# Cutting the first store of a streaming grouped 1x1 convolution into three parts

## The chip, the core and the metric

The kernel runs on one core of one Trainium2 chip. The metric is device time in microseconds (us) of that core. Five runs of the kernel before gave 477.75 to 478.17 us, with a median of 478.06 us.

## The reference

The input x has 512 x 512 pixels of 192 bfloat16 channels, in four groups of 48. Every group is multiplied by its own 48 x 48 matrix; the kernel size k is 1, so there is no neighbourhood and no padding.

```python
for i in range(k):          # k = 1
    for j in range(k):
        out = out + jnp.einsum('bhwgc,gcd->bhwgd',
                               xg[:, i:i+H, j:j+W, :, :], w[i, j])
```

So 100.66 MB are read and 100.66 MB are written, and there is little arithmetic for each byte.

## The kernel before

**Columns.** The pixels are laid out over 128 partitions. One "column" is one pixel in each partition: 384 bytes a partition, 49,152 bytes in all. There are about 2,050 columns. Four columns are a "group" (514 groups), two groups are a "pair" (257 pairs).

**Way of a group.** The SP queue loads columns into an input ring of 240 columns (`ring`). TensorE transposes a group in six blocks (L350) into `xT_ps`, VectorE copies a pair to `xT_sb` (L409), TensorE multiplies with block-diagonal weights (L370) into `o_ps`, and ScalarE (ACT) copies the group into an output ring of 280 columns, `oring` (L446). Stores go from `oring` to HBM and are issued by ACT too (L427), between two of its copies.

**Loads.** Loads are cut into pieces. The first three are 8, 24 and 48 columns (`HEAD`), and the later ones are mostly 80, that is 30,720 bytes a partition. SP waits on `t_done` until the transposes have freed the place in the ring (L318).

**Stores.** `plan_stores` cuts the output columns into stores whose ends lie on a grid of 72, 140, 212 and 280 columns of the ring (`OGRID`). For the last 240 columns the stores become smaller: 40 columns, and at the very end 24, 20, 16 and 8 (`LAST_PARTS`). The stores of the kernel before start with 72, 68, 72 and 68 columns. ACT issues a store while it handles a later group: at group g it first waits for the matmuls of g, then issues every store whose last group is at most g - 2 (L441), then waits for the store that last used this place in `oring` (L443), and then copies. So the first store of 72 columns (groups 0 to 17) is issued at group 19.

**Special fields.** At two places 48 columns are loaded and stored with uneven parts, some of them through the POOL queue (`PARTIAL`, `UNEVEN`), so that the 16 DMA engines get unequal shares. Nothing of this depends on the first store: POOL waits on `t_done`, and on `go_sem`, which ACT raises when it issues the stores of those fields.

**Queues.** Three queues feed the same 16 DMA engines: q1 (SP, the loads), q10 (ACT, the stores) and q0 (POOL, the uneven parts). A transfer over 128 partitions gives each engine 8 packets, one for each partition. Instructions are fetched over q8 and q14.

Of the kernel before, what the change touches and what calls it, by code (L numbers as in the profile page):

```python
# [1 line left out]

# [25 lines left out]
OGRID = (72, 140, 212, 280)  # L28
OCOLS = OGRID[-1]
HEAD = (8, 24, 48)  # L30
LATE_COLS = 240
LATE_PART = 40
LAST_PARTS = (24, 20, 16, 8)
# [50 lines left out]
def plan_fields(npix):  # L84

    parts, head = [], sum(HEAD)
    for slots, special in FRONT:
# [14 lines left out]
def plan_pieces(fields):  # L102
    pieces = []
    for f in fields:
        first = [f.cols]
        if f.full:
            first = list(HEAD) if not f.g0 and sum(HEAD) <= f.cols else []
        c = 0
# [7 lines left out]
def plan_stores(fields):  # L116
    total = 4 * fields[-1].g1
    stores, at = [], 0
    for f in fields:
        c = 0  # L120
        if not f.full and at + f.cols > OCOLS:
            at = 0
        ends = []
        if f is fields[-1] and f.cols > LATE_COLS:
            ends = [f.cols - sum(LAST_PARTS[i:]) for i in range(len(LAST_PARTS))]
        while c < f.cols:
            if f.full:
                end = min([g for g in OGRID if g > at + 24] or [OCOLS]) - at + c
                if f.cols < BIG:
                    end = min(OCOLS - at + c, f.cols)  # L130
                if ends and c >= f.cols - LATE_COLS:
                    end = min(OCOLS - at, LATE_PART) + c
                end = min([end, f.cols] + [e for e in ends if e > c])
            else:
                end = f.cols
            stores.append(Store(f, c, end, at))
            c, at = end, (at + end - c) % OCOLS
    return stores
# [40 lines left out]
def bass_standalone__grouped__vision_kernel(nc, x, w, out):  # L179
# [5 lines left out]
    fields = plan_fields(npix)  # L185
    pieces = plan_pieces(fields)
    stores = plan_stores(fields)
    units = plan_units(pieces)
    unit_of = {g: u for u in units for g in range(u.g0, u.g1)}
# [291 lines left out]
```

## Time and profile before

| what | value |
|---|---|
| median of 5 runs | 478.06 us (477.75 to 478.17) |
| the profiled execution | 478.44 us |
| its span, first to last instruction | 476.6 us, so 1.84 us lie around it |
| busy: PE, PEld, DVE, ACT | 432.2, 391.3, 246.8, 388.9 us |
| DMA queues q1, q10, q0, share of 16 engines | 48.0%, 47.8%, 3.3% |
| moved | 201.57 MB, 423 GB/s on the mean |
| granted TensorE clock | 0.971 on the mean |

A queue's share is the time that its packets took, summed over the engines and divided by 16 times the span. An engine works on one packet at a time, so these shares add up. The page's DMA line is the same in 40 slices of 11.9 us. A window's DMA share can be over 1.00, since a packet is counted in the window in which it starts.

### The profile page before, as it was taken

What the parts mean: (1) busy time and instruction counts of PE and PEld (TensorE: products, weight loads), DVE (VectorE), ACT (ScalarE), POOL (GpSimd) and SP (SyncE); (2) the same over time, 40 slices, a digit from 0 to 9 for tenths busy, and PEclk for the clock granted to TensorE, in tenths of its full rate; (3) what the DMA queues carried; (4) which work ended last, traced back from release to release, by engine and by line L of the source; (5) the groups of instructions that cost most, each with busy time, mean ns of one, the idle gap of its engine ahead of it and who ended that gap; (6) DMA issues with size and microseconds to landing.
All of it is one profiled execution on the core that took longest, in us unless ns stands there. A gap on an engine that the chain in (4) does not pass through costs nothing.

```text
span 476.6 us, 13580 instructions
## 1 busy us (share of the span) xinstructions
PE 432.2 (91%) x6178; PEld 391.3 (82%) x6178; DVE 246.8 (52%) x258; ACT 388.9 (82%) x515; POOL 12.5 (3%) x28
## 2 busy tenths in 40 slices
PE   4999999999698999999997997999978998996993
PEld 4988889888697898888897896898877987886882
DVE  2555555555354555555553553555535555552551
ACT  2898899988587998998894985999968987976883
POOL 1000000200002000000000000200002000000000
PEclk9999999999899999999997997999989999998998
DMA  8999999999999999999999999999999999999997
GB/s 324 442 384 428 441 426 430 436 418 436 439 430 424 435 420 438 437 429 425 441 432 429 429 431 431 431 430 422 435 441 419 433 422 424 440 424 432 420 419 291
DMA packets 10674, 201.57 MB, mean 423 GB/s; under 512 B 2112, under 2 KB 2112, under 8 KB 2752
## 3 DMA queue, kind: packets, MB, share of 16 engines
q1 hardware_dynamic: 4320, 97.44, 48.0%
q10 hardware_dynamic: 5120, 97.42, 47.8%
q0 software_dynamic: 1216, 6.49, 3.3%
q8 instruction: 9, 0.15, 0.1%
q14 instruction: 9, 0.07, 0.0%
HBM read 100.68 MB, written 100.66 MB: 422 GB/s over the span
## 4 chain that ended last, share of the span: by engine, by line
PE 48%; DMA 39%; ACT 9%; issue 1%; ACTq 1%; another core or an unknown queue 1%; SPq 0%; POOLq 0%
DMA out_dram<-oring 30%; PE o_ps L370 28%; PE xT_ps L350 20%; DMA ring<-in_x_dram 9%; ACT oring L446 9%; ACTq L427 1%; SPq L320 0%; SPq L313 0%; ACTq L420 0%; POOLq L300 0%; POOLq L299 0%; ACTq L429 0%
## 5 line engine op out<-in xcount | busy, mean ns | idle before, releaser
L446 ACT CAST oring<-o_ps 128x768 bf16<-128x768 f32 x514 | 387.6, 801 | 80.2 <-PE o_ps L370 56.6
L409 DVE COPY xT_sb<-xT_ps 128x1536 bf16<-128x1536 bf16 x257 | 246.2, 958 | 216.9 <-PE xT_ps L350 216.9
L370 PE MATMUL o_ps<-wt,xT_sb 128*128 128x144 bf16 (+1 forms) x3084 | 290.1, 237 | 26.5 <-ACT oring L446 21.0
L370 PEld LDWEIGHTS o_ps<-wt,xT_sb 128*128 128x128 bf16 x3084 | 213.7, 99 | 64.4 <-ACT oring L446 55.1
L350 PE MATMUL xT_ps<-ident,ring 128*128 128x128 bf16 x3084 | 223.1, 223 | 7.2 <-POOLq L300 3.9
L350 PEld LDWEIGHTS xT_ps<-ident,ring 128*128 128x128 bf16 x3084 | 190.9, 100 | 10.0 <-POOLq L300 4.1
L286 POOL DMA_DIRECT2D fill<-in_x_dram x8 | 4.6, 574 | 350.9 <-PE xT_ps L350 235.8
L296 POOL DMA_DIRECT2D ring<-in_x_dram x6 | 3.3, 559 | 0.0
L307 POOL DMA_DIRECT2D out_dram<-oring x6 | 3.3, 556 | 0.0
L332 PE MATMUL o_ps<-w_sb,esel 48*128 48x48 bf16 x10 | 0.6, 209 | 2.8 <-DMA w_sb<-in_w_dram 2.8
L332 PEld LDWEIGHTS o_ps<-w_sb,esel 48*128 48x128 bf16 x10 | 0.4, 111 | 2.7 <-issue 2.7
L402 DVE CAST wt<-o_ps 128x480 bf16<-128x480 f32 x1 | 0.7, 658 | 3.4 <-PE o_ps L332 3.4
L446 ACT ACT_TABLE_LOAD x1 | 1.3, 1283 | 0.8 <-PEq L466 0.8
L273 POOL TENSOR_SCALAR_AFFINE_SELECT esel<-esel 48x272 bf16<-48x272 bf16 x1 | 0.4, 402 | 0.0
L270 POOL MEMSET esel<- 48x272 bf16 x1 | 0.3, 318 | 0.3 <-POOLq L466 0.3
L277 POOL TENSOR_SCALAR_AFFINE_SELECT ident<-ident 128x128 bf16<-128x128 bf16 x1 | 0.3, 282 | 0.0
L271 POOL MEMSET ident<- 128x128 bf16 x1 | 0.2, 198 | 0.0
L466 POOL MEMSET const-float32-0.0<- 128x1 f32 x1 | 0.1, 98 | 0.3 <-issue 0.3
L466 POOL MEMSET const-bfloat16-1.0<- 128x1 bf16 x1 | 0.1, 101 | 0.0
L466 POOL MEMSET const-uint8-127<- 128x1 uint8 x1 | 0.1, 101 | 0.0
L466 POOL MEMSET const-float32-1.0<- 128x1 f32 x1 | 0.1, 98 | 0.0
## 6 DMA issues: line engine op xcount, KB each, us to landing
ring<-in_x_dram SPq DMA_DIRECT2D x22, 3840.0 KB, 26.8
out_dram<-oring ACTq DMA_DIRECT2D x11, 3456.0 KB, 41.3
out_dram<-oring ACTq DMA_DIRECT2D x10, 3264.0 KB, 41.5
out_dram<-oring ACTq DMA_DIRECT2D x3, 1920.0 KB, 19.6
out_dram<-oring ACTq DMA_DIRECT2D x1, 3840.0 KB, 47.5
ring<-in_x_dram SPq DMA_DIRECT2D x2, 1536.0 KB, 31.5
out_dram<-oring ACTq DMA_DIRECT2D x2, 1536.0 KB, 43.4
out_dram<-oring ACTq DMA_DIRECT2D x1, 2880.0 KB, 39.1
```

The lines of the kernel that those rows point to most:

```text
L273: gp.affine_select(out=esel[:], in_=esel[:], pattern=[[-1, ECOLS]], compare_op=AluOpType.is_equal, fill=0.0, base=ESHIFT, channel_multipli ...
L286: gp.dma_start(dst, src).then_inc(fill_sem[k], 16)
L296: gp.dma_start(sbuf, dram).then_inc(ld_sem[ld_key[p.i, n]], 16)
L307: gp.dma_start(dram, sbuf).then_inc(st_sem[i][n], 16)
L332: last = pe.matmul(o_ps[:, NOB - 1, col:col + CG], lhsT=esel[:, s0:s0 + 128], rhs=w_sb[:, g, :], start=True, stop=True, skip_group_check=True)
L350: last = pe.transpose(xT_ps[:, g % NXP, j * 128:(j + 1) * 128], xg[:, j * 128:(j + 1) * 128], ident[:])
L370: last = pe.matmul(o_ps[:, v % NOB, c0_:c1_], lhsT=xs[:, j * 128:(j + 1) * 128], rhs=wt[:, WOFF[tc]:WOFF[tc] + (c1_ - c0_)], start=(tc == ...
L402: dve.tensor_copy(wt[:], o_ps[:, NOB - 1, 0:WCOLS]).then_inc(wc_sem, 1)
L409: dve.tensor_copy(xT_sb[pair % NXS][:, 0:n * 2 * UC].rearrange("p (g c) -> p g c", g=n), xT_ps[:, b0:b0 + n, 0:2 * UC]).then_inc(e_done[pa ...
L427: act.dma_start(dram, sbuf).then_inc(st_sem[i][n], 16)
L446: act.copy(out_columns(g).rearrange("p (u c) -> p u c", u=2), o_ps[:, v % NOB:v % NOB + 2, 0:UC]).then_inc(fa_done[g % (2 * NTOK)] if g < ...
L466: nc = _bacc.Bacc("TRN2", target_bir_lowering=False, num_devices=1)
```

## The change

A new constant gives the sizes of the first parts, and `plan_stores` adds their ends, 8, 32 and 72, for the first field. The condition for the late stores is written out, as `ends` is no longer empty for the first field. Two more stores, two more semaphores and two more waits arise; from column 72 on the stores are those of before. The first part is ready with group 1, so ACT issues it at group 3; the second at group 9; the third at group 19, where the whole was issued before. Where the output ring comes round, ACT waits for the three parts at groups 70, 72 and 78 in place of one at group 70.

```diff
+from itertools import accumulate
...
+FIRST_STORES = (8, 24, 40)
...
-        ends = []
+        ends = list(accumulate(FIRST_STORES)) if not f.g0 and f.cols > OCOLS else []
         if f is fields[-1] and f.cols > LATE_COLS:
-            ends = [f.cols - sum(LAST_PARTS[i:]) for i in range(len(LAST_PARTS))]
+            ends += [f.cols - sum(LAST_PARTS[i:]) for i in range(len(LAST_PARTS))]
         while c < f.cols:
             if f.full:
                 end = min([g for g in OGRID if g > at + 24] or [OCOLS]) - at + c
                 if f.cols < BIG:
                     end = min(OCOLS - at + c, f.cols)
-                if ends and c >= f.cols - LATE_COLS:
+                if f is fields[-1] and f.cols > LATE_COLS and c >= f.cols - LATE_COLS:
                     end = min(OCOLS - at, LATE_PART) + c
                 end = min([end, f.cols] + [e for e in ends if e > c])
```

## The prediction, made before the changed kernel had run

> **What bounds the kernel now.** I read the page's time slices and queue table first.
>
> ```profile
> span 476.6 us, 13580 instructions
> ...
> PE   4999999999698999999997997999978998996993
> ...
> DMA  8999999999999999999999999999999999999997
> GB/s 324 442 384 428 441 426 430 436 418 436 439 430 424 435 420 438 437 429 425 441 432 429 429 431 431 431 430 422 435 441 419 433 422 424 440 424 432 420 419 291
> ...
> q1 hardware_dynamic: 4320, 97.44, 48.0%
> q10 hardware_dynamic: 5120, 97.42, 47.8%
> q0 software_dynamic: 1216, 6.49, 3.3%
> ```
>
> The DMA line is full in every slice but the first and the last, and the queues' shares add up to 99.1% of 16 engines. The engines are therefore never short of work between the first load and the tail, loads alone included: there is no hole at the start that an earlier store could fill. PE's line has gaps; it is busy 432.2 us of 476.6, so compute has 44 us to spare.
>
> Next the waits, ACT's alone, and ACT's timeline at the start and at the last long wait.
>
> ```profile
> ACT oring L446 <- PE o_ps L370: 56.6, 136, 8.3
> ACT oring L446 <- DMA out_dram<-oring: 16.9, 7, 4.9
> ```
>
> ```profile
> 12.79 3.06 ACT L446 CAST oring<-o_ps 128x768 bf16<-128x768 f32 x4 [0.80 <-PE o_ps L370]
> ...
> 25.86 0.80 ACT L446 CAST oring<-o_ps 128x768 bf16<-128x768 f32 x1 [0.20 <-PE o_ps L370]
> 26.34 0.38 ACTq L427 DMA_DIRECT2D out_dram<-oring  x1
> 26.76 2.28 ACT L446 CAST oring<-o_ps 128x768 bf16<-128x768 f32 x3
> ```
>
> ```profile
> 431.48 1.50 ACT L446 CAST oring<-o_ps 128x768 bf16<-128x768 f32 x2 [4.88 <-DMA out_dram<-oring]
> ...
> 469.97 0.34 ACTq L427 DMA_DIRECT2D out_dram<-oring  x1
> ```
>
> The first store is issued at 26.34 us. ACT waits seven times for a store to land so that `oring` has room, last at 431.48, and then runs to the last issue at 469.97. Last, the windows around the first store and at the end.
>
> ```profile
> 24.00:28.00 4.00, 3.74 (x56) 3.33 (x55) 2.62 (x3) 3.63 (x6) 0.00 (x0) 1.00 0.93 396
> 28.00:32.00 4.00, 3.97 (x64) 3.69 (x62) 1.92 (x2) 3.65 (x6) 0.00 (x0) 1.00 1.04 342
> 32.00:36.00 4.00, 3.97 (x62) 3.58 (x60) 2.47 (x3) 3.53 (x6) 0.00 (x0) 1.00 1.08 465
> ...
> 470.00:472.00 2.00, 0.00 (x0) 0.00 (x0) 0.00 (x0) 0.00 (x0) 0.00 (x0) 1.00 0.97 398
> 472.00:474.00 2.00, 0.00 (x0) 0.00 (x0) 0.00 (x0) 0.00 (x0) 0.00 (x0) 0.73 0.63 259
> 474.00:476.60 2.60, 0.00 (x0) 0.00 (x0) 0.00 (x0) 0.00 (x0) 0.00 (x0) 0.50 0.08 32
> ```
>
> The last two columns are DMA share and GB/s. After 28 us the rate falls to 342 with the engines busy; at the end they run dry one after another. The packet records of the trace, followed along one engine (each starts where the one before ended), show the first:
>
> ```
> start us, queue, bytes, ns
> 27.01 q1  30720 1138
> 28.15 q1  30720 1666
> 29.81 q1  30720 1736
> 31.54 q10 27648 1025
> 32.57 q10 27648 1025
> 33.59 q1  30720 1138
> 34.72 q10 27648 1025
> ```
>
> Two things are to be seen. Just before the first store packet two load packets take longer, by 1.13 us here; over all engines 29 load packets that start between 28.0 and 30.4 us are lengthened by 15.9 us, 1.00 us an engine. And from then on an engine takes one packet of each queue in turn, whatever their sizes. Along the engine that ends last (475.67 us, landing 476.1) the packets have no gap from 2.6 us on. So its sum of packet times is the kernel's time, and an edit costs what it adds to that sum.
>
> **Part by part.** *More and smaller packets.* A row of 27,648 bytes takes 1025 ns; rows of 3,072, 9,216 and 15,360 take 121, 347 and 573, together 1041. That is 16 ns more for a row, 8 rows an engine: 0.13 us. Two more stores end with two more 4-byte packets of 9 ns: 0.02. Sum +0.15 us, on the path, with no cover.
>
> The Trainium skill speaks against this edit: "DMA: Bandwidth & Descriptors", in "Rules for kernel authors", asks for at least 1 MiB in a DMA, and its fit in "Anatomy of one DMA" has about 2.0 us fixed for each. The parts of 192 and 576 KB are under that, and by the fit two more stores would be an estimated +4.0 us, 482.1 us. The trace does not agree where the queue is full: the last store, of 192 KB, goes through the last engine in 8 packets of 121 ns with no gap to the store ahead.
>
> *The stall ahead of the first store packet* (1.00 us). It comes about 13 us earlier now, with packets of 3,072 bytes. The one stall in the trace is near one 27,648-byte packet (1.03 us) in size. If it goes with the packet, 0.12 is left, a gain of 0.88. If it goes with the start of the queue, it is paid as before: 0. If every larger size pays once, 0.12 + 0.35 + 0.57 = 1.04 us: a loss of 0.04. If each of the three parts paid a full one, the loss is 2.00; against this stands that store packets go on without a pause from the first part on (below), and that later changes of size (12,288 to 23,040 and 27,648 bytes, from 180 to 220 us) show no lengthening over 0.04 us an engine in 10 us. I take a gain of 0.4, half way between gone and kept, as no row tells these two apart; -0.88 and +2.00 stay as ends.
>
> *Where the stores lie.* ACT copies groups 2 to 5 from 12.79, so part one is issued near 13.6, part two near 18.5, part three at 26.3. The first store's packets began 4 to 5 us after the issue; without its stall, the first part's begin near 17. With one packet of each queue in turn, eight rounds are 8 x (1.138 + 0.121) = 10.1 us, then 8 x 1.485 = 11.9, then 8 x 1.711 = 13.7. The 72 columns are through at about 52.7 us; before, they landed at 48.0 on the median engine. So the stores begin earlier and come through later: at 4.25 columns/us, loads are then some 20 columns ahead of before, and stores 20 behind. The engines' sums do not change by this: 0 us.
>
> What this makes late next: ACT's waits for `oring` can end up to 20 / 4.25 = 4.7 us later in the middle, covered by compute's 44 us. The last one counts most. The loads' last landing was 435.1 us; at 431.4 about half of the remaining 3.7 us was loads, so even if all loads go first, this store lands 1.9 us later, ACT goes on at 433.4 and issues the last store at 471.9. The last issue of before was followed by its first packets 1.55 us later, at 471.52, and the last engine came to it at 474.72: 3.2 us of cover. Cost 0, and 1 us for each us beyond 3.2.
>
> *ACT's two more issues*, 0.34 to 0.38 us each, stop its copies at groups 3 and 9; PE then waits 0.23 us, as at 27.6 us. Behind them only copies are queued. Without the 44 us of cover they would cost 0.8. The loads of columns 80 to 160 landed by 23.7 us; some 5 store packets of 0.121 us between them make it 24.3, and PE wants them at 24.57. The extra waits at groups 70 to 78 (about 69 us) find stores landed at 53. SP's and POOL's queues carry nothing new.
>
> Sum: +0.15 - 0.4 + 0 = -0.25 us on the profiled 478.44 (476.6 and 1.84 around it); that run lies 0.38 over the median, so I set it against the median: 478.06 - 0.25 = 477.8 us. A measurement of this kernel can tell about 0.2%, 0.96 us.
>
> **Rivals.** *Compute ends too late (slower).* The last engine's cover of 3.2 us is used up if ACT resumes later than 434.7 instead of 431.48. For it: ACT was held there for 4.88 us by the slowest engine alone. Against it: the bound of 1.9. If the whole lag of 4.7 us reached the end, 4.7 - 3.2 + 0.15 = +1.65: 479.7 us.
>
> *Each part pays the full stall (slower).* +2.00 + 0.15: 480.2 us. For it speaks the one stall; against it the quiet rows later.
>
> *The start is worth more (faster).* The stall goes but for 0.12: -0.88 + 0.15, 477.3 us. Beyond this, the last engine ends 1.07 us after the next one (474.60), having an instruction fetch of 0.97 us at 469.54; should that fall on another engine, 476.3 (477.3 - 1.07). It would take both to pass 0.2%; PE's code is not touched, which speaks against the second.
>
> *Nothing moves.* If store packets wait behind all queued loads, only +0.15 is left: 478.2.
>
> **How the numbers follow.** Within 0.2% lie my forecast, nothing moves (478.2), and a stall that goes without the fetch moving (477.3): 0.68 together. The two slower rivals have 0.09 each, 0.18 together. The faster one, past 0.2%, has 0.14. The range leaves one in ten on each side: 476.9 lies between 477.3 and 476.3, and 479.4 takes in most of a late end and half of the extra stalls.
>
> **What would show it.** Right: q10 packets of 3,072 bytes from about 17 us, one between two loads; the third part landing near 52 us; DMA slices as full as now; ACT's waits for stores longer than 16.9 us; the last landing on the same engine without a gap. Wrong: lengthened load packets before each part; a last store issued after 473 us with engines idle before it; or a slice with less DMA between 13 and 60 us.

## The result, and the profile after

The changed kernel takes 479.86 us (median of 38 runs, 477.50 to 481.98); the kernel before took 478.13 us on the same chips (64 runs, 476.84 to 481.31). The ratio is 1.0032, with a 95% interval of 1.0023 to 1.0042. By the ratio that is 1.5 us slower, more than the 0.2% that can be told, and the median lies 0.5 us beyond the upper end of the predicted range. The runs of either kernel scatter over some 4 us, so a single profiled execution shows a part of this. The one below took 479.08 us, 0.64 more than the profiled execution of before.

The page of the changed kernel, the lines that answer to those shown of before:

```profile
span 477.3 us, 13584 instructions
...
PE   5999999999989969999988998899978999996993
...
DMA  8999999999999999999999999999999999999996
GB/s 330 441 418 420 426 426 431 430 426 434 431 429 431 430 424 430 426 439 427 428 431 435 430 423 422 426 429 430 423 437 429 431 417 439 423 431 429 424 418 288
...
q1 hardware_dynamic: 4320, 97.44, 48.0%
q10 hardware_dynamic: 5408, 97.42, 47.8%
q0 software_dynamic: 1216, 6.49, 3.3%
```

The DMA engines are as full as before and move the same bytes, and the third GB/s slice, with the first store's packets in it, rose from 384 to 418. Nothing here says why the time grew. The waits of ACT and its timeline say a little more:

```profile
ACT oring L448 <- PE o_ps L372: 50.7, 134, 7.7
...
ACT oring L448 <- DMA out_dram<-oring: 24.2, 10, 5.5
```

```profile
11.94 0.38 ACTq L429 DMA_DIRECT2D out_dram<-oring  x1
...
17.11 0.34 ACTq L429 DMA_DIRECT2D out_dram<-oring  x1
...
25.99 0.34 ACTq L429 DMA_DIRECT2D out_dram<-oring  x1
...
178.93 0.80 ACT L448 CAST oring<-o_ps 128x768 bf16<-128x768 f32 x1 [5.49 <-DMA out_dram<-oring]
...
432.82 1.50 ACT L448 CAST oring<-o_ps 128x768 bf16<-128x768 f32 x2 [4.97 <-DMA out_dram<-oring]
...
471.34 0.34 ACTq L429 DMA_DIRECT2D out_dram<-oring  x1
```

The three parts are issued at 11.9, 17.1 and 26.0 us. ACT's waits for landed stores grew from 16.9 us (7 times) to 24.2 (10 times). In the kernel before, the first of them ended at 237 us:

```profile
237.32 0.80 ACT L446 CAST oring<-o_ps 128x768 bf16<-128x768 f32 x1 [0.82 <-DMA out_dram<-oring]
```

Now one of 1.0 us ends at 158.7, and one of 5.49 at 178.9. The last ends 1.3 us later than before, and the last store is issued at 471.34 instead of 469.97. The windows at both ends, with DMA share and GB/s last:

```profile
24.00:28.00 4.00, 3.60 (x55) 3.34 (x56) 1.92 (x2) 3.25 (x6) 0.00 (x0) 1.00 1.06 426
28.00:32.00 4.00, 3.97 (x63) 3.65 (x60) 2.13 (x3) 3.65 (x5) 0.00 (x0) 1.00 0.93 396
32.00:36.00 4.00, 3.97 (x62) 3.63 (x60) 2.65 (x3) 3.54 (x5) 0.00 (x0) 1.00 1.02 434
...
470.00:472.00 2.00, 0.10 (x2) 0.00 (x0) 0.00 (x0) 1.10 (x2) 0.00 (x0) 1.00 0.80 325
472.00:474.00 2.00, 0.00 (x0) 0.00 (x0) 0.00 (x0) 0.00 (x0) 0.00 (x0) 1.00 0.93 378
474.00:477.30 3.30, 0.00 (x0) 0.00 (x0) 0.00 (x0) 0.00 (x0) 0.00 (x0) 0.55 0.17 67
```

The dip of 342 GB/s at 28 to 32 us is gone (396). At the end some engines run dry before the last store, as the share of 0.80 shows.

**Where the time went.** The packet records show where, on the mean over the engines. Call a packet "lengthened" by the time that it took above the shortest of its size in that execution. Summed and divided by 16 engines, in us by stretches of the execution:

| execution | its time | sum | 0–60 | 60–180 | 180–300 | 300–440 | 440 on |
|---|---|---|---|---|---|---|---|
| before | 478.44 | 4.40 | 2.10 | 0.52 | 0.35 | 1.06 | 0.32 |
| after | 479.08 | 5.02 | 1.59 | 0.81 | 1.05 | 1.19 | 0.33 |
| after, on another occasion (first experiment) | 480.06 | 6.02 | 1.63 | 0.83 | 1.09 | 2.17 | 0.25 |

Without the lengthened part, the packets took 468.8 us an engine in the first two executions and 468.4 in the third. Against the execution of before, the two of after have 0.62 and 1.62 us more of lengthened packets, and took 0.64 and 1.62 us more; that the second pair agrees so well is chance, as the unlengthened part is 0.4 us smaller there. The first 60 us gained 0.5 us, as hoped; the 400 us behind them lost 1.1 and 2.1. So, on the mean over the engines, the loss does not lie where the change was made. The mean alone does not give the time of an execution. Among the kernels below, the whole store at group 27 had 4.41 us of lengthened packets, as much as before, in 479.33 us, and the three parts with stores of 104 behind them had 5.03 in 477.84 us. What counts is the engine that ends last, followed further below.

### The profile page after: what moved, and what is told of

Read it like the earlier page. It is cut to its first block, busy times and chain, and to the rows that moved or that the text cites. A ratio compares the mean times of both kernels' runs of the same rounds, so it can differ in the third digit from the quotient of the medians.

```text
span 477.3 us, 13584 instructions
## 1 busy us (share of the span) xinstructions
PE 430.2 (90%) x6178; PEld 389.2 (82%) x6178; DVE 246.8 (52%) x258; ACT 389.1 (82%) x515; POOL 12.5 (3%) x28
## 4 chain that ended last, share of the span: by engine, by line
DMA 54%; PE 35%; ACT 7%; another core or an unknown queue 1%; ACTq 1%; issue 1%; SPq 0%
DMA out_dram<-oring 49%; PE o_ps L372 20%; PE xT_ps L352 15%; ACT oring L448 7%; DMA ring<-in_x_dram 5%; ACTq L429 1%; SPq L322 0%; SPq L315 0%; ACTq L422 0%; ACTq L431 0%
```

## The experiments

Each ratio is to the kernel before, run on the same chip at the same time. "L" is the number of columns loaded and "S" of columns stored, by the packets of q1 and q10, at a given time. At 60 us L was 359 and S 121 in the profiled execution of before, 384 and 101 in that of after: the loads were 45 columns further ahead. "Lead" below means this distance, L less S, above that of before.

**The change again, its parts, and its order.** One kernel was the changed one. One began with parts of 8 and 64 columns. In the third, the three parts were all issued from group 19 on, when the whole store used to be issued. In the fourth, the store was whole and waited until group 27.

```diff
 # second
-FIRST_STORES = (8, 24, 40)
+FIRST_STORES = (8, 64)
 # third, on the changed kernel
-                while todo and stores[todo[0]].g1 <= g - 1:
+                while todo and stores[todo[0]].g1 <= g - 1 and (todo[0] > 2 or g >= 19):
 # fourth, on the kernel before
-                while todo and stores[todo[0]].g1 <= g - 1:
+                while todo and stores[todo[0]].g1 <= g - 1 and (todo[0] > 0 or g >= 27):
```

> The changed kernel once more, for a second profile and a comparison of many rounds with the kernel before. Theory 'lead': the packets of the small parts take turns with 30,720-byte load packets, so the 72 columns land later (50.8 to 52.8 us against 48.0 to 49.6), loads run some 20 to 25 columns ahead of before, ACT waits longer for the output ring (24.2 us against 16.9 in the first profile), the load queue runs dry at times, and the end comes later: +1.0 to +2.0 us, ACT's waits over 20 us again, last store issued after 470.5 us. Theory 'start': the cost lies in the first 60 us, in lengthened packets; +1.0 to +2.0 us as well, but lengthened packets in the first 60 us exceed those of before (2.1 us an engine).

> Two parts, 8 and 64 columns. The first is issued at group 3 as in the changed kernel, but the 72 columns need 16 rounds in place of 24: 8 x 1.259 + 8 x (1.138 + 0.914) = 26.5 us from about 17, so they land near 44 to 47 us, before those of the kernel before (48.0 to 49.6). Theory 'lead': loads are not ahead (358.5 columns or fewer at 60 us), ACT's waits stay at or under 16.9 us, and the time is that of before, -0.6 to +0.4 us. Theory 'start' (an early, small first store costs by itself): +0.8 to +2.0 us.

> The three parts of 8, 24 and 40 columns, all issued at group 19, where the whole store of before was. No early start, only the small packets. Theory 'lead': 24 rounds from about 31 us, so the 72 columns land at about 66 us and loads run further ahead than in the changed kernel, until the input ring is full: +1.5 to +4 us, ACT waiting over 24 us. Theory 'start': without the early start there is only the cost of smaller packets, 0 to +0.4 us.

> The kernel before with its first store of 72 columns whole, but issued at group 27 in place of 19: about 6.5 us later, so it lands at about 55 us. No early start and no small packet, only stores that lie further behind the loads (some 28 columns, about as in the changed kernel). Theory 'lead': +1.0 to +2.5 us, ACT waiting over 20 us. Theory 'start': 0, within 0.4 us.

| edit | median, us | ratio | L, S at 60 us |
|---|---|---|---|
| three parts again | 480.02 | 1.0030 [1.0013, 1.0048] | 390, 95 |
| 8 and 64 | 477.74 | 0.9999 [0.9983, 1.0014] | 357, 129 |
| three parts, late | 479.85 | 1.0046 [1.0027, 1.0066] | 400, 85 |
| whole, at group 27 | 479.74 | 1.0039 [1.0021, 1.0058] | 392, 94 |

The early start falls as the cause: 8 and 64 columns start as early and cost nothing that can be told, and two kernels that start no earlier lose as much as the change. Small parts fall too, since the fourth has none. What the losing kernels share is the lead: loads at 384 columns or more at 60 us, against 357 to 359. A late last store, the prediction's first rival, falls as the common cause too. The executions of 480.06 us (three parts again) and 481.59 us (three parts, late) issued theirs at much the same time as the kernel before, 469.97 us:

```profile
470.19 0.34 ACTq L429 DMA_DIRECT2D out_dram<-oring  x1
...
469.99 0.37 ACTq L429 DMA_DIRECT2D out_dram<-oring  x1
```

**Loads held back.** SP got one more wait. At the load piece named in `HOLDS` it waits for 8 pairs of groups (64 columns) more than the ring needs. Two kernels had it on the kernel before, at piece 14 (some 172 us) or at 13, 16 and 19. A third run changed the grid of the output ring to 240 columns, so that stores came back to ACT sooner.

```diff
+HOLDS = (14,)
...
-                if freed(p) > seen:
-                    seen = freed(p)
+                hold = 8 if p.i in HOLDS else 0
+                if freed(p) + hold > seen:
+                    seen = freed(p) + hold
...
 # the third, on the kernel before
-OGRID = (72, 140, 212, 280)
+OGRID = (80, 160, 240)
```

> The kernel before with one load held back: for load piece 14 SP waits for 8 pairs of transposes more (about 13 us), so that the load queue runs empty once, near 215 us, for some 5 us. Loads are then less far ahead, not further. Theory 'empty load queue': in the trace of the three parts issued at group 19 an engine whose load queue had been empty took about 1.2 us longer over the next packets and often 0.7 to 0.8 us again some 14 us later, so this costs +0.6 to +2.0 us. Theory 'late end' (loads that run ahead make ACT wait for the output ring, and the last store is issued too late): ACT's waits fall below 16.9 us, and the time is that of before, within 0.5 us.

> The same for load pieces 13, 16 and 19, so three empty spells of the load queue. Theory 'empty load queue': about two to three times the cost of one hold, +1.5 to +5 us, and lengthened packets of 5.5 us or more an engine (before: 4.4). Theory 'late end': within 0.7 us, with ACT's waits shorter still.

> The kernel before with an output ring of 240 columns cut into three stores of 80, so that store and load packets have the same 30,720 bytes and take turns evenly; the loads' lead, which grows from 239 to 375 columns between 50 and 300 us in the kernel before, should stay near 240. Theory 'empty load queue': the input ring never fills, the load queue stays full, lengthened packets after 60 us fall under the 2.3 us an engine of before, -1.2 to +0.2 us. Theory 'late end': with a smaller output ring ACT waits longer and the time is +0.5 us or more.

One hold: 477.27 us, 0.9981 [0.9963, 1.0000]. Three: 477.55, 0.9986 [0.9970, 1.0002]. With one hold the load queue ran empty (no load packet started from 174 to 178 us), and yet the kernel was not slower; the waits of ACT fell by half:

```profile
ACT oring L448 <- DMA out_dram<-oring: 9.0, 5, 2.5
```

So an empty load queue is not dear in itself. The smaller ring took 487.64 us, 1.0194 [1.0156, 1.0232]. It is a case of its own. Its profiled execution, at 483.15 us well under the median, has packets lengthened by 8.33 us an engine, and the last store issued at 476.31. Most of its engines ran dry before the small stores at the end, which is what compute that comes late looks like; the lengthened packets are there as well, and what each is worth was not separated:

```profile
472.00:474.00 2.00, 1.61 (x22) 1.23 (x21) 0.96 (x1) 2.00 (x4) 0.00 (x0) 1.00 0.83 340
474.00:476.00 2.00, 1.02 (x12) 0.61 (x10) 0.00 (x0) 1.74 (x3) 0.00 (x0) 1.00 0.65 259
476.00:478.00 2.00, 0.00 (x0) 0.00 (x0) 0.00 (x0) 0.28 (x1) 0.00 (x0) 0.53 0.99 402
```

PE and ACT still work at 474 to 476 while the engines are at 0.65. In the changed kernel both had stopped by 472.

**Three parts with larger stores behind them.** After the three parts, the rest of the first field was stored in parts of 104 columns, to win the lead back.

```diff
-FIRST_STORES = (8, 24, 40)
+FIRST_STORES = (8, 24, 40, 104, 104)
...
+                if f is fields[0] and c < sum(FIRST_STORES):
+                    end = f.cols
```

> The changed kernel with its three parts, followed by two stores of 104 columns in place of 68, 72 and 68 (the rest of the first lap of the output ring). Their packets of 39,936 bytes take turns with load packets of 30,720, so the stores regain what the small parts lost: 280 columns stored at about 94 us, against 255 to 260 before. Early start, small packets and the two more stores are all kept. Theory 'lead' (with either way in which it becomes time): the time of the kernel before, -0.6 to +0.4 us. If the parts cost by themselves at the start: +1.0 to +2.0 us as in the changed kernel.

479.40 us, 1.0025 [1.0001, 1.0050]: not clear. The lead was gone by 100 us (L less S 240 there, 264 in the kernel before), and the kernel was still slower, if barely. Its profiled execution took 477.84 us, well under the median, and cannot show why.

**The lead taken back.** The wait of SP, now on the changed kernel, at piece 7 (some 62 us) or at piece 14; then the kernel with 8 and 64 columns with the wait at 14; then the kernel before with one hold again.

> The changed kernel, but SP waits for 8 pairs (64 columns) more before it issues load piece 7, at about 70 us. The three parts and the early start stay; only the lead of the loads over the stores is taken away, soon after it arose. Theory 'lead': what the change costs comes from the loads lying 25 to 40 columns further ahead; with 64 columns taken back the loss is gone: 477.0 to 478.4 us, ratio 0.998 to 1.0008, and from 180 us on load packets lengthened as in the kernel before or less (at most 1.8 us an engine from 180 us to the end; the changed kernel had 2.6 to 3.5). Rival 'late landings': the three parts cost through the later landing of column 72 and what waits for it before 70 us, which the hold does not undo: 479.4 to 480.2 us, ratio 1.0025 to 1.0045. Second rival 'hold itself': a hold this early leaves the stores alone for a while and PE short of columns, and what this costs shows as a load queue that is empty and a rate below 400 GB/s: over 480.2 us.

> The changed kernel with the same wait at load piece 14 (about 172 us), as in the kernel before with one hold (0.998 of the kernel before). 'Lead': the lead of 60 to 170 us stays and what it costs there (lengthened packets 0.3 us an engine more than before), the greater part later goes: 477.3 to 478.5 us, ratio 0.9985 to 1.001. 'Late landings': the hold takes away as much as it did in the kernel before, 0.9 us, from the changed kernel's 479.9: 478.8 to 479.3 us, ratio 1.0015 to 1.003.

> First parts of 8 and 64 columns (0.9999 of the kernel before) and one hold at piece 14 (0.9981). 'Lead': there is no lead in the parts of 8 and 64, so the two edits add: 477.0 to 477.7 us, ratio 0.997 to 0.999. 'Late landings' says the same; the run is there as a candidate for a faster kernel. If the hold's gain was chance, 477.7 to 478.3.

> The kernel before with one hold at piece 14, once more, as its interval (0.9963 to 1.0) touched no change. 'Lead': 0.997 to 0.9995, 476.9 to 477.8 us. If the gain was chance: 0.9995 to 1.001.

| edit | median, us | ratio |
|---|---|---|
| three parts, 8 pairs at piece 7 | 479.34 | 1.0032 [1.0010, 1.0055] |
| three parts, 8 pairs at piece 14 | 477.82 | 1.0009 [0.9992, 1.0027] |
| 8 and 64, 8 pairs at piece 14 | 477.22 | 0.9980 [0.9960, 0.9999] |
| kernel before, 8 pairs at piece 14 | 477.50 | 0.9996 [0.9984, 1.0007] |

The first was a miss for "lead". At 80 us L less S was 204, less than the 249 of before, and the whole loss was still there. The second goes with "lead", without excluding the rival. The last one shows that the gain of one hold, 0.9981 the first time, is about 0.1% over the two runs. No version was found that beats the kernel before by the 0.2% that can be told; 8 and 64 with one hold comes nearest.

**What the miss left open.** Half the wait (4 pairs, which puts the loads where they were before), the wait at piece 7 in the kernel before, both waits in the changed kernel, and half of the delay of the whole store.

```diff
 # first, on the changed kernel with HOLDS = (7,)
-                hold = 8 if p.i in HOLDS else 0
+                hold = 4 if p.i in HOLDS else 0
 # second, on the kernel before
-                while todo and stores[todo[0]].g1 <= g - 1:
+                while todo and stores[todo[0]].g1 <= g - 1 and (todo[0] > 0 or g >= 23):
 # third, the kernel before with HOLDS = (7,); fourth, the changed one with
+HOLDS = (7, 14)
```

> The changed kernel with a wait for 4 pairs (32 columns) more at load piece 7. With 8 pairs the columns loaded less stored fell by 95 at 80 us (299 to 204), so with 4 they come to about 250, where the kernel before had 249. Theory 'lead': the place of the loads is that of the kernel before from 80 us on, so the loss goes: 477.6 to 478.5 us, 0.9993 to 1.001. Rival 'late landings' (what the parts cost lies before 70 us or does not depend on the lead): 479.3 to 480.0 us, 1.0025 to 1.004. Theory 'late dry spells' (the loss comes when the load queue runs empty after a wait of ACT of over 4 us for a store, at 179 or 388 us, and the load packets are lengthened as it fills again): no price from the lead alone; the time follows whether the profile shows such a wait before 430 us.

> The kernel before, its first store whole but issued from group 23 on instead of 19 (group 27 gave 1.0039). 'Lead' with a loss that grows in step: about half, 478.7 to 479.3 us, 1.0015 to 1.0025. If the loss sets in at a certain lead (ACT waits for stores before 200 us or not): either under 1.001 with ACT's first wait after 230 us, or 1.003 to 1.0045 with one at 160 to 180 us.

> The kernel before with the wait for 8 pairs at load piece 7: the control for the run with the three parts and this wait (1.0032). If the wait costs something itself: 1.002 to 1.004, 479.0 to 480.0 us, and the lead stays a cause. If the wait costs nothing here, as at piece 14: 0.998 to 1.0005, 477.0 to 478.3 us; then the three parts cost what they cost without a lead, and 'lead' falls.

> The changed kernel with both waits, at pieces 7 and 14. If all that matters is the load packets lengthened after 180 us (at most 0.2 us on the engine that ends last with the wait at piece 14 in the kernel before, 1.7 with the wait at piece 7 here): 477.0 to 478.0 us, 0.998 to 1.0005. If the parts cost something that no wait cures: 478.8 to 479.6 us, 1.0015 to 1.003.

| edit | median, us | ratio |
|---|---|---|
| three parts, 4 pairs at piece 7 | 478.61 | 0.9998 [0.9981, 1.0014] |
| whole, at group 23 | 480.98 | 1.0060 [1.0038, 1.0083] |
| kernel before, 8 pairs at piece 7 | 478.77 | 1.0008 [0.9990, 1.0027] |
| three parts, 8 pairs at 7 and 14 | 477.96 | 1.0006 [0.9992, 1.0020] |

Half the wait brings L less S at 80 us to 261 (249 before), and the loss is gone by the ratio, with all three parts still there. This is the best answer here to what the parts cost by themselves: 0.14% at most, with whatever the wait itself gains or costs in it. Its runs fall into two groups, five of 477.1 to 477.8 us and seven of 478.6 to 479.2, and the medians (478.61 against 478.04 of the kernel before) would give 1.0012. The whole store at group 23 has a smaller lead than at group 27 (L less S 274 against 298 at 60 us) and loses more, not half, which is outside all that was expected. So the loss does not grow in step with the lead. It also says, without any small part, that the place of the first store alone is worth up to 0.6%. The wait at piece 7 in the kernel before lies between both expectations; it may cost up to 0.27%, which could explain a part of the loss that it left in the changed kernel. Both waits together give 1.0006, just above the 1.0005 that was expected at most if lengthened packets after 180 us are all that matters, and below the 1.0015 of a cost that no wait cures, though the interval reaches over that.

**Which engine, which packets.** Where the records of all 16 engines could be put in order to the end, the engine that ends last can be followed. In each of these executions it is one that also fetched two pieces of instructions of 16,384 bytes. The sums take the packets that start after 12 us; as each packet starts 3 to 4 ns before the one ahead of it ends, 2.3 us in all, they come to some 10 us less than the end:

| execution | its time | ends | unlengthened | lengthened | of that from 60 us to 440 | idle |
|---|---|---|---|---|---|---|
| three holds | 477.24 | 474.52 | 462.15 | 2.04 | 0.17 | 0 |
| one hold | 477.38 | 474.61 | 462.10 | 2.04 | 0.17 | 0 |
| one hold, again | 477.77 | 475.04 | 462.04 | 2.47 | 0.26 | 0 |
| 8 and 64, hold 14 | 477.89 | 475.14 | 462.12 | 2.50 | 0.96 | 0 |
| 8 and 64 | 477.83 | 475.11 | 461.61 | 3.14 | 1.21 | 0 |
| three parts, 4 pairs at 7 | 477.83 | 475.22 | 461.73 | 3.46 | 1.36 | 0 |
| three parts, 8 pairs at 7 and 14 | 477.67 | 475.04 | 462.19 | 2.38 | 1.02 | 0 |
| before | 478.44 | 475.67 | 462.14 | 3.02 | 1.50 | 0 |
| three parts, 8 pairs at 7 | 479.25 | 476.49 | 462.24 | 3.66 | 1.23 | 0.51 |
| three parts, late | 481.59 | 478.98 | 461.70 | 7.13 | 4.72 | 0 |

The work of this engine is 461.6 to 462.2 us in each of them, so its end moves with the lengthened packets and, in one, the idle time. In the late three parts, 1.15 us came at 40 us, 1.25 at 204, 0.80 at 220 and 0.95 at 413. Of these packets, more of them loads than stores, some lie where one queue had run short on that engine and rejoins the other: three packets of q10 in a row stand before the one at 205 us. At 220 us eight packets that took turns stand before it, so this is not the whole of it. The changed kernel's records could be followed to 472 us only; up to there seven of its engines have no gap. So for the change itself the engine that ends last is not shown. The best fit to its records has an engine with two such fetches end last, at 476.4 us without a gap, with 2.2 us of lengthened packets from 60 to 440 us (1.50 in before). As the records of two engines can be exchanged at some places on this way, that is an estimate.

**A wait that goes with it.** The longest wait of ACT for a store that ends before 430 us, in each profiled execution with the ring of 280 columns:

| longest wait, us (its end) | the execution's time, us |
|---|---|
| 7.62 (389), three parts again | 480.06 |
| 7.09 (392), kernel before, 8 pairs at 7 | 484.37 (the longest of 13 runs, median 478.77) |
| 6.34 (388), three parts, 8 pairs at 7 | 479.25 |
| 6.25 (389), three parts late | 481.59 |
| 5.49 (179), after | 479.08 |
| 4.92 (225), whole at 23 | 479.71 |
| 3.67 (288), 8 and 64 | 477.83 |
| 3.44 (290), whole at 27 | 479.33 |
| 3.39 (255), before | 478.44 |
| 3.34 (256), three parts, 4 pairs at 7 | 477.83 |
| 1.5 to 3.3, the seven others so far | 477.24 to 478.70 |

All six with over 4 us took 479.08 or more; of the others all but one took 478.70 or less. The execution of 484.37 is a poor witness: in its last 5.6 us a single engine was at work, where the others had ended. What such a wait does can be read in the windows of the changed kernel (PE's busy time and matmuls, its clock, DMA share and GB/s):

```profile
174.00:176.00 2.00, 0.30 (x5) 0.09 (x2) 0.88 (x1) 0.00 (x0) 0.00 (x0) 1.00 1.02 434
176.00:178.00 2.00, 0.00 (x0) 0.00 (x0) 0.00 (x0) 0.00 (x0) 0.00 (x0) 0.85 0.90 376
178.00:180.00 2.00, 0.22 (x2) 0.22 (x3) 0.00 (x0) 1.07 (x2) 0.00 (x0) 0.50 1.07 460
180.00:182.00 2.00, 2.00 (x20) 1.98 (x19) 0.00 (x0) 1.23 (x2) 0.00 (x0) 0.50 1.02 438
182.00:184.00 2.00, 2.00 (x19) 1.96 (x17) 0.96 (x1) 1.12 (x2) 0.00 (x0) 0.50 0.98 416
184.00:186.00 2.00, 2.00 (x33) 1.94 (x32) 0.96 (x1) 1.38 (x3) 0.00 (x0) 0.95 1.02 435
```

PE stops with ACT, and its granted clock is 0.50 from 177.4 to 184.2 us, with 20 matmuls in 2 us instead of 33. Transposes are late, input columns are freed late, and at 200 to 202 us only 2 load packets start where 16 did before. From 214 to 220 us packets are lengthened, by 0.21 us an engine (0.02 in before). Is the stop the cause, or a sign? Two kernels put one into the kernel before: ACT copies one group eight times, each copy waiting for the one before, at group 186 or 405.

```diff
+STALL = 405
 # 186 in the other kernel
...
+        x_sem = sem("x_sem")
...
+                for k in range(7 if g == STALL else 0):
+                    act.copy(out_columns(g).rearrange("p (u c) -> p u c", u=2),
+                             o_ps[:, v % NOB:v % NOB + 2, 0:UC]).then_inc(x_sem, 1)
+                    act.wait_ge(x_sem, k + 1)
```

> The kernel before, ACT copies group 405 (about 386 us) eight times instead of once, each waiting for the one before: a stop of some 6 us for PE, as long as the waits of 6.2 to 7.6 us at 388 us in three of the slower kernels. Theory 'stop': such a stop before the loads are through makes PE late, the load queue runs empty 12 to 20 us later and load packets are lengthened as it fills again: 479.0 to 480.2 us, 1.002 to 1.0045; two packets of loads or less in 2 us at 400 to 406 us, 0.5 to 1 us more of lengthened packets an engine after 400 us. Rival 'sign': PE has 44 us to spare, the stop is hidden: 477.7 to 478.5 us, 0.9993 to 1.001, and no dry load queue there.

> The same at group 186 (about 177 us), where the changed kernel waited 5.49 us. 'Stop': load queue empty near 200 us, lengthened packets in 180 to 300 us up from 0.35 to 0.7 us an engine or more; 478.8 to 480.0 us, 1.0015 to 1.004. 'Sign': 477.7 to 478.5 us, 0.9993 to 1.001. If the stop only takes away lead, as a wait at load piece 14 did: 477.0 to 477.8 us, 0.998 to 0.9993.

Group 186: 477.85 us, 1.0003 [0.9984, 1.0022]. Group 405: 478.67 us, 1.0010 [0.9994, 1.0026]; its stop fell at 370 us, earlier than meant. The windows of the first show the stop that was wanted:

```profile
174.00:176.00 2.00, 0.00 (x0) 0.00 (x0) 0.58 (x1) 1.94 (x3) 0.00 (x0) 1.00 1.06 452
176.00:178.00 2.00, 0.00 (x0) 0.00 (x0) 0.00 (x0) 1.94 (x3) 0.00 (x0) 0.58 0.97 410
178.00:180.00 2.00, 0.99 (x8) 0.93 (x9) 0.00 (x0) 1.62 (x3) 0.00 (x0) 0.50 1.00 430
180.00:182.00 2.00, 2.00 (x20) 1.97 (x19) 0.00 (x0) 1.60 (x2) 0.00 (x0) 0.50 1.07 459
```

No load packet started at 188 to 190 us and only 3 at 206 to 208, yet packets were lengthened by 0.41 us in 180 to 300 us (0.35 in before), and by 0.21 on the last engine from 180 to 440 us. At 177 us the stop, the halved clock and the dry load queue together cost nothing that can be told (0.22% at most), so there a stop alone does not make the loss. At 370 us the run is undecided; its profiled execution had 1.79 us of lengthened packets from 300 to 440 us (1.06 in before).

**What stays open.** Shown is what brings the loss on: a first store that comes through later, cut or not (1.0030 to 1.0060 in four kernels), unless the loads are then held back (0.9998 to 1.0009 with three of the four waits tried on the changed kernel, 1.0032 with the fourth). Shown is also what does not by itself: the early start, the parts, a stop at 177 us, an empty load queue. The place of the loss, lengthened packets after the first 60 us, is shown for the changed kernel on the mean over the engines, and for the ten executions of the table on the engine that ends last. Not shown is what makes a packet or two take 1 us longer in one case and almost nothing in another. Nor is it shown why group 23 loses more than group 27, or why 64 columns taken back at 62 us did not help where 32 did. That the engines are out of step with one another then is a guess.

## Why the prediction was wrong

**The step that failed** is "Where the stores lie", with its last sentence, "The engines' sums do not change by this: 0 us." What it said of the places came true: store packets began at 15.5 us (17 foreseen), the first, second and third part landed by 26.7, 38.7 and 52.8 us (72 columns foreseen at 52.7), and the loads were 25 columns further on at 60 us (some 20 foreseen) with 20 fewer columns stored (20). The price of these places was taken as nothing, as if no order of the packets changed their sum. That holds for the unlengthened times, 468.8 us an engine in the first two executions. It does not hold for the lengthened ones: after the first 60 us they were 2.30 us an engine in before (4.40 less 2.10), and 3.43 and 4.39 in the two executions of after. So the term that was put at 0 measured 1.1 and 2.1 us on the mean over the engines; why these packets take longer stays open. The trace of before had them in view, 2.30 of 4.40 us, and the prediction looked at the first stall alone.

**More and smaller packets: +0.15.** The durations were those of before, 121, 347 and 573 ns, so the term stands as worked out. The measured price of three parts, with the loads where they were (half the wait at piece 7), is 0.9998 [0.9981, 1.0014], at most 0.7 us. The Trainium skill's fit in "DMA: Bandwidth & Descriptors", "Anatomy of one DMA", with about 2.0 us fixed for each DMA, would have made it an estimated +4.0 us; the section gives it for DMAs issued by gpsimd (POOL), while ACT issues these stores, and this run excludes it for them where the queue is full. The sizes in the prediction are half the real ones: at 49,152 bytes a column, the parts of 8, 24 and 40 columns are 384, 1,152 and 1,920 KB, so only the first is under 1 MiB, and the last store is 384 KB as well. The term of 0.15 does not rest on them.

**The stall ahead of the first store: -0.4.** Right by 0.1 on the mean over the engines: lengthened packets in the first 60 us fell by 0.51 us in the profiled execution and 0.47 in the other. On the engine that ends last no gain is shown: from 12 to 60 us it had 1.0 us of them in before and, in the fit above, 1.2 in after.

**Waits of ACT and the cover at the end: 0.** Right in its bounds. The last wait ended at 432.82 (433.4 at most foreseen) and the last issue came at 471.34 (471.9). Some engines ran dry there, the share of 0.80 at 470 to 472 us; the last landing, at 476.9, came 5.6 us after this issue.

**ACT's two more issues** show as 0.38 and 0.34 us at 11.94 and 17.11, with no loss behind them: the kernel with 8 and 64, which has one of them, is at 0.9999.

**The rivals.** Two slower ones gave times close to the result, 479.7 and 480.2 us, for reasons that did not happen. "Compute ends too late" needed ACT to resume after 434.7; it did at 432.8. "Each part pays the full stall" needed lengthened packets before each part; the first 60 us have less of them, not more. Of the five signs under "What would show it" four were on the side of right: the packets of 3,072 bytes, the third part's landing, full slices, longer waits. The fifth, the last landing on the same engine without a gap, is only estimated above. None of them could show the loss, as none looks at how long the packets after 60 us take. The chance of 0.18 for slower held mechanisms at the two ends of the kernel and none for its middle.

## What to carry to other kernels

With full DMA engines, an edit that only moved transfers was not free here, even where their sizes stayed (1.0039 and 1.0060). Sum, for the engine that ends last, the time of its packets above the shortest of their size over the whole span, not only around the edit; a part of it that lies elsewhere can change with the phase of loads and stores, that is, with how far the loads are ahead. In the ten executions above that time, from 12 us on, ranged from 2.0 to 7.1 us, and the loss did not grow in step with the lead, so judge a cut of the first store also with the phase restored (here, by holding the loads back by 32 columns). A long wait in a slow execution may be a sign: put the same wait in alone before taking it for the cause.

## What the runs showed that was not expected

- A stop of PE of 5.4 us, with 6.8 us at a granted clock of 0.50 and an empty load queue 10 us later, cost nothing that can be told at 177 us (1.0003). In the changed kernel, with the stop at group 186 and with the one at 405, the clock fell 3.1, 2.7 and 4.7 us after PE's last matmul, stayed at 0.50 for 6.8 us each time, and was back 4.4, 4.2 and 5.7 us after the next matmul. The Trainium skill, "TensorE: Matmul & The Clock Gate", Part 1, gives at least one window of about 3.4 us, idle for the fall and busy for the return; two of the three falls came sooner than that here, and all returns later.
- A whole first store that is issued 4 groups later (at group 23) costs 0.60%, and 8 groups later (at 27) 0.39%; both move the loads ahead, by 36 and 60 columns of L less S at 60 us.
- One of the 16 engines carries far more lengthened packets than the others (some 18 us with three parts and 8 pairs at piece 7, some 20 with 8 and 64 and the hold) and still does not end last, as the kernel gives engines uneven shares and its unlengthened packets take some 20 us less. In the ten executions of the table the end is set by an engine with two fetches of instructions.
